# A layernorm + MLP kernel: the first weight piece moves from SP's DMA queue to ACT's, and four matmuls move ahead of the third tile's transposes

## The chip, the cores and the metric

The kernel runs on one core of a Trainium2 chip. The core has TensorE (PE: matmuls, and transposes as matmuls against an identity), VectorE (DVE), ScalarE (ACT), GpSimd (POOL) and SyncE (SP), and 16 DMA engines that all queues share. The metric is the device time of one execution in microseconds (us), lower is better; the time before is the median of 3 runs.

## What is computed

```python
def reference(x, w1, b1, w2, b2):            # x 1x2048x1024, w1 1024x3584, w2 3584x1024, all bf16
    y = _layernorm(x, axis=-1)
    h = _gelu(jnp.einsum("bsd,df->bsf", y, w1) + b1)
    return jnp.einsum("bsf,fd->bsd", h, w2) + b2
```

## The kernel before

**Tiling.** The 2048 rows of x are 16 tiles of 128 rows, in four blocks of 512 rows (four tiles). D = 1024 is 8 slices of 128 (`dt`), F = 3584 is 28 rows of 128 (`r`). For each block, the first matmul makes 28 rows of hT (128 features x 512 tokens), each accumulated over 8 `dt` in one PSUM bank; ACT applies gelu; the second matmul accumulates the 28 rows into 128x512 output pieces, DVE adds b2 and SP stores.

**The queues.** The program is five hand-ordered lists of instructions, one per engine; each instruction carries the events that it waits for. An engine never overtakes its own list. DVE's list in the steady part is put together by a planner from estimated ready times (`est`), which sums of matmul times and DMA bytes feed.

**The start.** PE runs 25 matmuls on a constant (L471), transposes b1 (L512), and then the first three tiles of x, which are multiplied raw, without their layernorm ("RAW", tiles 0, 1, 2); mean and rstd are put right afterwards on DVE (L529, L536, L539). `pe_T` (L320) transposes one tile in 8 transposes (L336, 128x128 each) into two PSUM banks, and ACT copies each bank to `yT_sb` (L352); tiles 0 and 1 are cut 4 + 4, tile 2 is cut 2 + 6. Tile 2 uses the banks of tile 0 again ("t" and "2_0"), so it waits for ACT's copies of these.

**The wave.** Then the first eight rows of hT are made as "cells" (`pe_wave`, L389, matmul L397): one cell is one row r and one slice dt over some tiles. A cell over tiles 0 and 1 has 258 columns (two columns of ones among them), over tile 2 128, over all three 386. The first weight piece, `w0`, holds rows 0 to 3 of dt 0 (128 KB), `w1` the same rows of dt 1, `w2` of dt 2 and 3, and so on (`PIECES`). Of piece 0 the four cells of tiles 0 and 1 come first, then the four of tile 2 (L564 to L567); all later pieces are cells of three tiles (L568), row by row. Tile 3 follows with 64 cells of 128 columns from its own normalised copy, and then come full rows (L382, 512 columns).

**The loads.** SP issues, in this order: x0, x1, x2 (256 KB each), w0, w1 (128 KB each), w2, w3, x3 (256 KB each) and so on; b1 (7 KB) alone is issued on ACT's queue (`issue`, L212; the DMA itself is recorded at L189). POOL's first instructions make the identity, a few constants and, for every tile, two memsets (L243, L244; the last is the event `eps15`).

**ACT's list at the start:** table load, b1's DMA, the copy of b1 out of PSUM (L516), the six copies of transposed tiles (L352), then the spreading of the means (L486), which waits for DVE until 11.2 us.

## Time and profile before

| | |
|---|---|
| median of 3 runs | 396.61 us (396.26 to 396.75) |
| the profiled execution: its time, its span | 396.67 us, 395.4 us |
| PE busy in the span | 390.9 us (99%) |
| DVE, ACT, POOL busy | 162.0, 86.2, 11.7 us |
| mean granted TensorE clock | 1.00 |
| first tile landed, first tile transposed, first cell | 3.5, 3.71, 6.38 us |

The span runs from the first recorded instruction to the last; 1.27 us of the execution lie outside it. Times in the timeline count from the start of the span. A timeline row is a start, a length to the end of the last instruction in the row, engine, line, operation, out<-in, shape and count. Matmuls overlap: one of 128 columns is recorded as 0.2 to 0.3 us long, so PE's pace is read from the distances of starts and not from lengths.

### The profile page before, as it was taken

How to read it: one execution, taken by the hardware profiler on the slowest of the kernel's cores; microseconds unless marked ns; L12 is line 12 of the kernel's file. 1: busy time of each engine (PE TensorE's matmuls, PEld its weight loads, DVE VectorE, ACT ScalarE, POOL GpSimd, SP SyncE). 2: the span in 40 equal slices, each digit the busy share in tenths (PEclk: the TensorE clock that was granted, in tenths of full speed). 3: DMA queues.
4: the chain of work that ended last, by engine and by line, in shares of the span. 5: the costliest groups of instructions: out<-in, count | busy, mean ns of one | idle time of the engine just before them, and what ended most of it. 6: DMA issues, size and time to landing. Idle time of an engine off the chain costs nothing.

```text
span 395.4 us, 4518 instructions
## 1 busy us (share of the span) xinstructions
PE 390.9 (99%) x1904; PEld 184.9 (47%) x1938; DVE 162.0 (41%) x338; ACT 86.2 (22%) x139; POOL 11.7 (3%) x59
## 2 busy tenths in 40 slices
PE   9999999999999999999999999999999999999998
PEld 7744444444444444444444444444444444444444
DVE  5998889988999306987100000001100000001011
ACT  3655420000144332000023443100003334400000
POOL 3101000011001100000000000000000000000000
DMA  7999940000000000000000000000000000000000
GB/s 257 373 385 386 387 155 26 16 27 14 28 0 0 2 0 0 28 26 15 28 13 2 0 0 2 13 13 28 25 15 15 0 0 2 0 15 27 13 28 27
DMA packets 16078, 23.63 MB, mean 60 GB/s; under 512 B 1082, under 2 KB 8250, under 8 KB 16058
## 3 DMA queue, kind: packets, MB, share of 16 engines
q1 hardware_dynamic: 16016, 23.33, 16.7%
q8 instruction: 15, 0.25, 0.3%
q14 instruction: 5, 0.04, 0.0%
q10 hardware_dynamic: 42, 0.01, 0.0%
HBM read 19.14 MB, written 4.19 MB: 59 GB/s over the span
## 4 chain that ended last, share of the span: by engine, by line
PE 99%; issue 0%; DVE 0%
PE ps L449 49%; PE ps L382 38%; PE ps_t L382 7%; PE ps L397 3%; PE ps L471 1%; PE ps_t L397 0%; PE ps L336 0%; PE ps_t L336 0%; DVE o_sb L460 0%; PE ps L512 0%
## 5 line engine op out<-in xcount | busy, mean ns | idle before, releaser
L449 PE MATMUL ps<-w_sb,hT_sb 128*128 128x512 bf16 (+2 forms) x909 | 193.3, 373 | 0.8
L382 PE MATMUL ps<-yT_sb,w_sb 128*128 128x512 bf16 x678 | 152.4, 379 | 0.9
L449 PEld LDWEIGHTS ps<-w_sb,hT_sb 128*128 128x128 bf16 x924 | 88.6, 98 | 105.2
L407 ACT ACTIVATE hT_sb<-ps,b_sb 128x512 bf16<-128x512 f32 x94 | 64.0, 687 | 234.4 <-PE ps L382 217.2
L382 PEld LDWEIGHTS ps<-yT_sb,w_sb 128*128 128x128 bf16 x696 | 68.0, 98 | 81.9
L460 DVE TENSOR_TENSOR o_sb<-ps,b_sb 128x512 bf16<-128x512 f32 (+2 forms) x33 | 22.3, 675 | 198.7 <-PE ps L449 198.5
L304 DVE STREAM_TRANSPOSE yT_sb<-x_sb 32x256 bf16<-32x256 bf16 x192 | 83.7, 436 | 21.9 <-PE ps_t L382 18.8
L382 PE MATMUL ps_t<-yT_sb,w_sb 128*128 128x512 bf16 x135 | 31.9, 379 | 0.1
L248 DVE BATCH_NORM_STATS2 st_sb<-x_sb 128x6 f32<-128x512 bf16 x32 | 21.0, 672 | 4.7 <-DMA x_sb<-in_x_dram 4.6
L382 PEld LDWEIGHTS ps_t<-yT_sb,w_sb 128*128 128x128 bf16 x136 | 13.3, 98 | 16.1
L407 ACT ACTIVATE hT_sb<-ps_t,b_sb 128x512 bf16<-128x512 f32 x18 | 12.4, 687 | 17.5 <-PE ps_t L382 14.6
L397 PE MATMUL ps<-yT_sb,w_sb 128*128 128x128 bf16 (+2 forms) x116 | 13.1, 269 | 0.0
L397 PEld LDWEIGHTS ps<-yT_sb,w_sb 128*128 128x128 bf16 x116 | 8.9, 98 | 3.5
L255 POOL TENSOR_TENSOR rstd_sb<-mv_sb,nhalf 128x1 f32<-128x1 f32 x13 | 7.1, 548 | 113.6 <-DVE mv_sb L258 113.6
L423 DVE TENSOR_TENSOR ps<-ps,row_r 128x384 f32<-128x384 f32 x17 | 9.2, 561 | 2.7 <-PE ps L382 2.5
L262 DVE TENSOR_SCALAR x_sb<-x_sb,mv_sb,rstd_sb 128x1024 bf16<-128x1024 bf16 x13 | 7.0, 541 | 2.0 <-POOL rstd_sb L255 1.3
L536 DVE SCALAR_TENSOR_TENSOR ps<-row_r,ncs,ps 128x384 f32<-128x384 f32 x7 | 4.2, 614 | 0.6 <-PE ps L397 0.6
L486 ACT COPY row_r<-row_r 32x384 f32<-32x384 f32 x6 | 3.1, 510 | 4.3 <-DVE row_r L480 4.2
L539 DVE TENSOR_TENSOR ps<-ps,row_r 128x384 f32<-128x384 f32 x7 | 3.9, 563 | 0.2
L529 DVE TENSOR_TENSOR yT_sb<-yT_sb,row_r 128x768 bf16<-128x768 bf16 x4 | 3.6, 950 | 0.0
L471 PE MATMUL ps<-const-bfloat16-1.0 128*128 128x128 bf16 x25 | 2.8, 309 | 0.8 <-PEq L679 0.8
L258 DVE BATCH_NORM_AGGREGATE mv_sb<-st_sb 128x2 f32<-128x15 f32 x13 | 2.9, 222 | 0.4
(34 smaller groups left out, 32.9 us busy)
## 6 DMA issues: line engine op xcount, KB each, us to landing
w_sb<-in_w_dram SPq DMA_DIRECT2D x4, 1792.0 KB, 18.3
w_sb<-in_w_dram SPq DMA_DIRECT2D x2, 2048.0 KB, 16.4
out_dram<-o_sb SPq DMA_DIRECT2D x31, 128.0 KB, 1.7
x_sb<-in_x_dram SPq DMA_DIRECT2D x3, 1024.0 KB, 14.4
w_sb<-in_w_dram SPq DMA_DIRECT2D x7, 256.0 KB, 5.4
x_sb<-in_x_dram SPq DMA_DIRECT2D x4, 256.0 KB, 3.4
w_sb<-in_w_dram SPq DMA_DIRECT2D x1, 1024.0 KB, 10.1
w_sb<-in_w_dram SPq DMA_DIRECT2D x2, 128.0 KB, 3.7
```

The costliest lines, as they stand in the source:

```text
L248: return (lambda e, i=i, h=h, pw=pw: e.bn_stats(st_sb[i][:, 6 * h:6 * (h + 1)], x_sb[:, i, h * pw:(h + 1) * pw]), [x_ev[i][h if len(x_ev[i ...
L255: pool.op(lambda e, i=i, dst=dst, mv=mv: e.tensor_tensor(out=dst, in0=mv[:, 1:2], in1=nhalf[:, i:i + 1], op=ALU.pow), waits=[f"mv{i}", "nh ...
L262: return (lambda e, i=i, c0=c0, c1=c1: e.tensor_scalar(out=x_sb[:, i, c0:c1], in0=x_sb[:, i, c0:c1], scalar1=mv_sb[:, i, 0:1], scalar2=rst ...
L304: res.append((lambda e, src=src, dst=dst: e.transpose(out=dst, in_=src), waits, (f"tr{i}" if lastop else None), 0.47))
L382: pe.op(lambda e, b=b, r=r, dt=dt, bank=bank: e.matmul(unit_bank(bank)[:, 0:TB], lhsT=w1_sb[:, dt, r * P:(r + 1) * P], rhs=yT_sb[:, ybuf(b ...
L397: pe.op(lambda e: e.matmul(unit_bank(bank)[:, n0:n1], lhsT=w1_sb[:, dt, r * P:(r + 1) * P], rhs=yT_sb[:, 0 if tiles[0] in RAW else ybuf(0) ...
L407: act.op(lambda e, r=r, n0=n0, n1=n1, bank=bank: e.activation(out=hT_sb[:, r, n0:n1], in_=unit_bank(bank)[:, n0:n1], func=ACT.Gelu_apprx_tanh,
L423: crit.append((est[sig], (lambda e, reg=reg: e.tensor_tensor(out=reg, in0=reg, in1=row_b(1), op=ALU.mult), [sig, "row_1"], ready, 0.57), 0))
L449: pe.op(lambda e, sl=sl, ft=ft, c0=c0, c1=c1, bank=bank: e.matmul(ps_2[:, bank, 0:c1 - c0], lhsT=hT_sb[:, ft, sl * P:(sl + 1) * P], rhs=w2 ...
L460: crit.append((est[sig], (lambda e, ob=ob, c0=c0, c1=c1, bank=bank: e.tensor_tensor(out=o_sb[:, ob, c0:c1], in0=ps_2[:, bank, 0:c1 - c0], ...
L471: pe.op(lambda e: e.matmul(ps_1[:, 0, 0:P], lhsT=ones, rhs=ones, start=True, stop=True))
L536: return [(lambda e: e.scalar_tensor_tensor(out=reg, in0=row_b(0), scalar=ncs[:, c:c + 1], in1=reg, op0=ALU.mult, op1=ALU.add), [f"m1_0_{r ...
```

## The change

- `w0` is issued on ACT's queue and not on SP's, behind b1's DMA, and it waits for POOL's last start-up memset (`eps15`). SP's queue issues x0, x1, x2, w1 and so on, all behind x2 one place earlier.
- Tiles 0 and 1 are cut 2 + 6 as tile 2 is. ACT's copies are ordered by piece: first piece of tile 0, first of tile 1, second of tile 0, second of tile 1.
- PE's order becomes: transposes of tiles 0 and 1; the four cells of dt 0 over tiles 0 and 1; the transposes of tile 2; the four cells of dt 1 over tiles 0 and 1; eight cells of tile 2 (dt 0 and 1); then cells of three tiles from dt 2 on. In before, dt 1 had cells of three tiles.
- Inside a piece the cells go slice by slice (all rows of one dt, then the next dt), and no more row by row.

```diff
-GROUPS_0 = (0, 4, 8)
-GROUPS_2 = (0, 2, 8)
+GROUPS = (0, 2, 8)
...
+N_EARLY = 1
+N_PAIR = 2
...
-SP_FIRST_LOADS = ("b1", "x0", "x1", "x2", "w0", "w1", "w2", "w3", "x3", "w4", "w5", "w6", "w7", "w8")
+SP_FIRST_LOADS = ("b1", "x0", "x1", "w0", "x2", "w1", "w2", "w3", "x3", "w4", "w5", "w6", "w7", "w8")
...
-                load_w1(int(item[1:]))
+                dma_q[0] = act if item == "w0" else sp
+                load_w1(int(item[1:]), [f"eps{NT - 1}"] if item == "w0" else [])
+                dma_q[0] = sp
...
+        def put_copy(i, groups, banks, k):
+            g0, g1 = groups[k:k + 2]
+            bname = banks[k]
+            assert banks.count(bname) == 1
+            src = bank_of[bname][:, 0:(g1 - g0) * P].bitcast(I32)
+            src = src.rearrange("p (j s) -> p j s", j=g1 - g0)
+            dst = yT_sb[:, 0, g0:g1, ycol(i):ycol(i) + P].bitcast(I32)
+            act.op(lambda e, dst=dst, src=src: e.copy(out=dst, in_=src), waits=[f"tp{i}_{k}"], sig=f"te{i}_{k}")
+            bank_read[bname] = f"te{i}_{k}"
...
-        pe_T(0, GROUPS_0, ("t", "2_0"))
-        pe_T(1, GROUPS_0, ("2_1", "1_4"))
-        pe_T(2, GROUPS_2, ("t", "2_0"))
-        put_row_spread(0, 1, 4)
+        T_BANKS = (("t", "2_0"), ("2_1", "1_4"), ("t", "2_0"))
+        for t in RAW[:2]:
+            pe_T(t, GROUPS, T_BANKS[t])
+        for k in range(2):
+            for t in RAW[:2]:
+                put_copy(t, GROUPS, T_BANKS[t], k)
...
-        first = [(r, dt) for r in PIECES[0][2] for dt in range(*PIECES[0][:2])]
-        for tiles in (RAW[:2], RAW[2:]):
-            for r, dt in first:
-                wave_cell(r, dt, tiles)
-        cells = [(r, dt) for j0, j1, rows in PIECES[1:] for r in rows if r < R for dt in range(j0, j1)]
+        cells_of = lambda a, b: [(r, dt) for j0, j1, rows in PIECES[a:b] for dt in range(j0, j1) for r in rows]
+        for r, dt in cells_of(0, N_EARLY):
+            wave_cell(r, dt, RAW[:2])
+        pe_T(2, GROUPS, T_BANKS[2])
+        for k in range(2):
+            put_copy(2, GROUPS, T_BANKS[2], k)
+        put_row_spread(0, 1, 4)
+        for r, dt in cells_of(N_EARLY, N_PAIR):
+            wave_cell(r, dt, RAW[:2])
+        for r, dt in sorted(cells_of(0, N_PAIR), key=lambda c: (c[1] >= GROUPS[1], c)):
+            wave_cell(r, dt, RAW[2:], f"raw_{r}" if dt == DT - 1 else None)
+        cells = cells_of(N_PAIR, len(PIECES))
```

More of the change, by code (lines that the diff above doesn't have):

```diff
@@ L117, in bass_standalone__mixer_channel_mlp__prompt_kernel @@
     assert NB1 + NB2 + 1 <= 8 and NB2 == 2
-    assert all(c[-1] == DT for c in (GROUPS_0, GROUPS_2, HALVES))
+    assert all(c[-1] == DT for c in (GROUPS, HALVES))
     assert TPB == 4 and RAW == (0, 1, 2)
@@ L201, in load_x_block, with load_w1 @@
                 x_ev[i] = (f"xb{b}", f"xb{b}")
-        def load_w1(ci):
+        def load_w1(ci, waits=()):
             j0, j1, a, b = w1_chunks[ci]
-            dma(w1_sb[:, j0:j1, a:b], w1v[:, j0:j1, a:b], f"w1c{ci}", (j1 - j0) * P * (b - a) * 2)
+            dma(w1_sb[:, j0:j1, a:b], w1v[:, j0:j1, a:b], f"w1c{ci}", (j1 - j0) * P * (b - a) * 2, waits)
             w1_issued.add(ci)
@@ L340, in pe_T @@
                     off += P
-            off = 0
-            prev = None
-            for k, (g0, g1) in enumerate(zip(groups[:-1], groups[1:])):
-                bname = banks[k]
-                if bname != prev:
-                    off = 0
-                prev = bname
-                done = max(m for m in range(len(banks)) if banks[m] == bname)
-                src = bank_of[bname][:, off:off + (g1 - g0) * P].bitcast(I32)
-                src = src.rearrange("p (j s) -> p j s", j=g1 - g0)
-                dst = yT_sb[:, 0 if i in RAW else ybuf(blk), g0:g1, ycol(i):ycol(i) + P].bitcast(I32)
-                act.op(lambda e, dst=dst, src=src: e.copy(out=dst, in_=src), waits=[f"tp{i}_{done}"],
-                       sig=f"te{i}_{k}")
-                off += (g1 - g0) * P
-                bank_read[bname] = f"te{i}_{k}"
-            pe_t[0] += DT * 0.056
+            pe_t[0] += DT * 0.056
+        def put_copy(i, groups, banks, k):
[7 more added lines that the diff above has]
+            bank_read[bname] = f"te{i}_{k}"
         unit_n = [0]
```

## Prediction, made before the result was known

> **What bounds the kernel now.** The page's chain of work first: it says which engine the end hangs on.

> ```profile
> ## 4 chain that ended last, share of the span: by engine, by line
> PE 99%; issue 0%; DVE 0%
> ```

> PE alone. So an edit is worth what it changes in PE's stream: a stall, or the pace. Next PE's timeline, to find where the stream isn't dense.

> ```profile
> 0.83 2.82 PE L471 MATMUL ps<-const-bfloat16-1.0 128*128 128x128 bf16 x25 [0.83 <-PEq L679]
> 3.58 0.20 PE L512 MATMUL ps<-ident,b1r_sb 28*128 28x28 bf16 x1
> 3.71 0.61 PE L336 MATMUL ps_t<-ident,x_sb 128*128 128x128 bf16 x4
> 4.11 1.49 PE L336 MATMUL ps<-ident,x_sb 128*128 128x128 bf16 x12
> 5.71 0.37 PE L336 MATMUL ps_t<-ident,x_sb 128*128 128x128 bf16 x2
> 5.87 0.67 PE L336 MATMUL ps<-ident,x_sb 128*128 128x128 bf16 x6
> 6.38 6.38 PE L397 MATMUL ps<-yT_sb,w_sb 128*128 128x258 bf16 x42
> ...
> 16.52 0.49 PE L397 MATMUL ps_t<-yT_sb,w_sb 128*128 128x386 bf16 x2
> 16.84 3.29 PE L397 MATMUL ps<-yT_sb,w_sb 128*128 128x128 bf16 x56
> 19.97 0.61 PE L397 MATMUL ps_t<-yT_sb,w_sb 128*128 128x128 bf16 x8
> ```

> Three readings, from starts. (a) Pace: the 12 transposes at 4.11 have 11 steps in 1.49 - 0.31 = 1.18 us, 107 ns for 128 columns; the 56 cells of 16.84 to 19.97 take 56 ns for as many columns. PE begins at half its later pace. The six transposes from 5.87 to 6.38 took 0.51 us: a of them at 107 and 6 - a at 56 gives a = 3.4, so the pace doubles at 5.87 + 3.4 x 0.107 = 6.23 us. The profile's column for the granted clock says 1.00 there, so only the steps show it. (b) One stall: the 16 transposes of tiles 0 and 1 would be followed by the next at 5.39 (3.71 + 16 steps, the first ones a little short); it comes at 5.71. (c) From 6.38 on nothing is lost: 34 cells of 386 columns at 163 ns, 4 of 258 at 110 and 4 of 128 at 56 are 6.2 us, and the row lasts from 6.38 to 12.60. Beyond that the steps stay 56 and 216 ns to the last matmul. So the change can act only on the first 6.4 us.

> What ended the stall, and whether it was the DMA: the queue and ACT.

> ```profile
> 1.69 0.42 SPq L189 DMA_DIRECT2D x_sb<-in_x_dram  x1
> x_sb<-in_x_dram SPq DMA_DIRECT2D x1, 256.0 KB, 3.9
> ...
> 2.15 0.43 SPq L189 DMA_DIRECT2D w_sb<-in_w_dram  x1
> w_sb<-in_w_dram SPq DMA_DIRECT2D x1, 128.0 KB, 3.8
> ```

> The first pair is x2: issued at 1.69, landed 3.9 later, 5.6. PE's next transpose starts 0.13 after that, while the bank that it also waits for had been copied by 4.73 (ACT's first copy, below). The stall is x2's. The second pair is w0: 2.15 + 3.8 = 5.95, needed at 6.38.

> ```profile
> 4.36 0.37 ACT L352 COPY yT_sb<-ps_t 128x256 int32<-128x256 int32 x1 [0.36 <-PE ps_t L336]
> 4.79 1.23 ACT L352 COPY yT_sb<-ps 128x256 int32<-128x256 int32 x3
> 6.11 0.27 ACT L352 COPY yT_sb<-ps_t 128x128 int32<-128x128 int32 x1
> 6.58 0.48 ACT L352 COPY yT_sb<-ps 128x384 int32<-128x384 int32 x1 [0.20 <-PE ps L336]
> ```

> **The change, part by part.**

> Transposes and copies. The same 24 transposes. Copies of tiles 0 and 1: four of 0.37 become two of 0.27 and two of 0.48, the same 1.5 us. By the same delays as in the rows above (0.04 behind PE, 0.05 apart) they run 4.15 to 4.41, 5.00 to 5.26, 5.31 to 5.79, 5.85 to 6.33. Tiles 0 and 1 have dt 0 in `yT_sb` at 5.26, before PE is through with their transposes (5.39): no wait. Tile 2 needs "2_0" free, 5.79, and will come later than that.

> w0 on ACT's queue. It waits for POOL's last memset, 2.29 + 0.09 = 2.38, and so is issued at about 2.42. ACT's one other issue took 0.62 us; the copy of b1 at 3.82 stands behind it, and ACT had 1.75 us idle before that: hidden, with 0.8 us of cover. SP's issues behind x2 start 0.47 earlier; the 16 DMA engines are full (DMA share 1.03 between 2.82 and 6.24), so bytes and not issues set when w1 and the rest land. I put this at nothing: no cell of these pieces waited.

> When w0 lands is the unknown price. Early end: 2.42 + 2.7, what x0 took with nothing ahead, = 5.1. Late end: 2.42 + 3.9, x2's own, = 6.3; short of that, 5.95 is where it lands today. With x1's 2.9 it would be 5.3. I take 5.4: nothing stands ahead on its queue, as with x1, but it shares the engines with the rest of x1 and with x2. x2 is then late by w0's share, 5.95 at most, as the two together are the bytes that are in by then today.

> [...]

> PE's new stretch. Let s be the start of the first early cell: the later of 5.39 and w0's landing + 0.13. From s to the end of piece 1, PE has 4 cells of 258 (0.44 us), 8 transposes (0.45), 4 cells of 258 (0.44), 8 cells of 128 (0.45): 1.78 us at full pace, and what runs before 6.23 goes at half. So the end is 6.23 + 1.78 - (6.23 - s)/1.95. In before the same point is 6.38 + 0.44 + 0.22 + 4 x 0.163 = 7.69.
> - w0 by 5.26: s = 5.39, end 7.58, gain 0.11.
> - w0 at 5.4: s = 5.54, end 7.65, gain 0.04.
> - w0 at 5.95: s = 6.08, end 7.93, loss 0.24.
> - w0 at 6.3: s = 6.45, end 8.23, loss 0.54.
> - No gain and no loss at w0 = 5.5.

> The gain is small for a plain reason: the stall that goes lies in the stretch of half pace, where 0.32 us of idle time are 0.16 us of work; and the cells put into it run at 215 ns and not at 110.

> Waits further on. With s = 5.54, the cells end at 6.32 and tile 2's transposes run 6.32 to 6.77, behind x2 (5.95 at most): its wait is gone. Its copies run 6.62 to 6.89 and 6.95 to 7.43; the cells that need them start at 7.21 and 7.65. Hidden, with 0.2 us of cover. w2 (landed 3.10 + 3.9 = 7.0) is needed at 7.65.

> Slice-by-slice order: the same cells. A change of bank costs no more than none: 163 ns holds for piece 1, which changes bank each cell, as for the pairs in one bank later. Row 0's end signal comes up to 1 us later, but ACT's reader waits for the last row anyway and stands behind copies that end at 12.8. Zero. Splitting dt 1's four cells costs 4 x (110 + 56 - 163) = 0.01, in the sum. The planner's estimates move by 0.01 us: at worst a few DVE instructions trade places, and PE waited for none of them in before.

> Later covers that a PE earlier by 0.1 us eats into: tile 3's copies end at 15.9, needed 16.8; the last bank of the wave is read by 28.76 and written again at 29.05. Both hold, so the gain reaches the end.

> **Sum.** Against the profiled execution: 396.67 - 0.04 = 396.63. It stands 0.06 above the median of 396.61, so against the median 396.57. What a measurement of this kernel can tell from no change is about 0.2%, 0.79 us; the whole bracket lies inside that.

> **The rivals.**

> 1. ACT's queue brings w0 no earlier than SP's did (the change doesn't do what it says). For: engines full, and issued 0.27 later than on SP. Against: b1's small load on that queue was in before PE asked for it at 3.58, while x1's load stood on SP's. Loss 0.24 (5.95) to 0.54 (6.3): 396.85 to 397.15. Chance 0.2.

> 2. The pace doubles sooner. Then w0 alone sets s: 5.54 + 1.78 = 7.32, gain 0.37, 396.24; with w0 at 5.1, s = 5.25, 7.03, gain 0.66, 395.95. For: the runs differ by 0.49 us with no stall beyond 6.4 to vary. Against: one trace, one doubling. Chance 0.14. [...]

> 3. The other side: the wait for w0 is long enough that PE doesn't count as busy, and the pace doubles later. PE had run 5.4 us (0.83 to 6.23), idle 0.45 of them, when it doubled. If a stall of 0.7 or more (w0 later than about 6.0) starts that count again at s = 6.2, the doubling comes at 11.6, and half of 11.6 - 6.23 is lost: 2.7 us, 399.3. For: half pace at first, so something is counted. Against: the 0.32 stall at 5.39 didn't prevent it, and w0 must be later than today. Chance 0.06. [...]

> **Numbers.** Forecast (w0 by 5.5, doubling near 6.2) 0.60, rivals 0.20, 0.14, 0.06. Faster by over 0.2% needs more than any case but an early doubling with an early load would give: 0.03. Slower: rival 3 and the tail of rival 1: 0.07. Same: 0.90. Range 396.0 to 397.0: from rival 2 to most of rival 1.

> **What would show it.** Step 1: w0's issue on ACT at 2.4 and landing 2.7 to 3.5 later. Step 2: no gap between the 16th transpose and the first cell of 258 columns beyond 0.2, at steps of 215 ns. Step 3: eight transposes behind the cells at 56 ns and no gap before them. Step 4: the first cells of 386 columns at 7.6 to 7.7 in place of 7.04 + 0.65. It would be wrong if the pace doubles elsewhere than at 6.0 to 6.5, if w0 lands after 5.6, or if PE waits anywhere beyond 8 us.

## The result, and the profile after

The changed kernel is slower by 0.3%: 397.12 us against 396.48 us (medians of 22 executions each); the ratio of the means is 1.0029, 95% interval 1.0018 to 1.0040. The forecast was 396.57 and no measurable difference.

The 22 executions fall into two groups, with nothing between 397.23 and 398.61. Fifteen lie at 396.86 to 397.23 (median 397.04, 0.56 above before); seven lie at 398.61 to 399.05 (median 398.90, 1.86 above the first group). Before had none of 22 there. The two together give the mean: 0.56 + 7/22 x 1.86 = 1.15 us, as 397.61 - 396.48 = 1.13. All 22 count in the comparison; what makes the second group is the subject of half the experiments. The profiled execution, 397.13 with a span of 395.9, belongs to the first; none of the second was traced. Its mean granted clock is known, though: 0.996 in two of the seven (399.01 and 399.05), 1.00 in the other five, as in all of the first group.

The page's chain of work, in 4, now holds a DMA:

```profile
PE 98%; DMA 1%; POOL 0%; issue 0%; DVE 0%; POOLq 0%
PE ps L447 49%; PE ps L380 38%; PE ps_t L380 7%; PE ps L395 3%; DMA w_sb<-in_w_dram 1%; PE ps_t L395 0%; POOL st_sb L247 0%; POOL st_sb L246 0%; PE ps L339 0%; POOL ident L239 0%; DVE o_sb L458 0%; PE ps_t L339 0%; POOL yT_sb L242 0%; POOL nhalf L243 0%; POOLq L239 0%
```

The chain in order of time says which DMA (start, length, what):

```profile
2.41 3.85 DMA w_sb<-in_w_dram
6.26 0.14 issue
6.40 0.60 PE ps L395 x4
```

That is w0: issued on ACT at 2.41 behind POOL's last memset (the small POOL entries above), landed at 6.26, and the early cells start at 6.40. PE's timeline of the same stretch, to be laid beside the one of before:

```profile
3.90 1.70 PE L339 MATMUL ps<-ident,x_sb 128*128 128x128 bf16 x14
6.40 0.60 PE L395 MATMUL ps<-yT_sb,w_sb 128*128 128x258 bf16 x4 [0.80 <-DMA w_sb<-in_w_dram]
6.84 0.27 PE L339 MATMUL ps_t<-ident,x_sb 128*128 128x128 bf16 x2
6.95 0.50 PE L339 MATMUL ps<-ident,x_sb 128*128 128x128 bf16 x6
7.28 5.46 PE L395 MATMUL ps<-yT_sb,w_sb 128*128 128x258 bf16 x39
```

Behind the 16th transpose PE could have gone on at 5.39; it stands until 6.40 (the 0.80 counts from the end of that transpose). In before the same place cost 0.31. The steps ahead of the wait are at half pace (the 14 transposes, 107 ns each), those behind it at full pace (the four cells 6.40 to 6.84, 110 ns each; the transposes behind them 56): the doubling fell into the wait. The first cell of 386 columns starts at 8.17, with the work done that before had done at 7.69 (its point behind piece 1): 0.48 later, and this stays to the last matmul (0.47).

### The profile page after: what moved, and what is told of

Its sections match the earlier page's. It is cut to its first block, busy times and chain, and to the rows that moved or that the text cites. A ratio compares the mean times of both kernels' runs of the same rounds, so it can differ in the third digit from the quotient of the medians.

```text
span 395.9 us, 4560 instructions
## 1 busy us (share of the span) xinstructions
PE 392.5 (99%) x1942; PEld 185.0 (47%) x1942; DVE 162.0 (41%) x338; ACT 86.1 (22%) x139; POOL 11.7 (3%) x59
## 4 chain that ended last, share of the span: by engine, by line
PE 98%; DMA 1%; POOL 0%; issue 0%; DVE 0%; POOLq 0%
PE ps L447 49%; PE ps L380 38%; PE ps_t L380 7%; PE ps L395 3%; DMA w_sb<-in_w_dram 1%; PE ps_t L395 0%; POOL st_sb L247 0%; POOL st_sb L246 0%; PE ps L339 0%; POOL ident L239 0%; DVE o_sb L458 0%; PE ps_t L339 0%; POOL yT_sb L242 0%; POOL nhalf L243 0%; POOLq L239 0%
## 5 line engine op out<-in xcount | busy, mean ns | idle before, releaser
L395 PE MATMUL ps<-yT_sb,w_sb 128*128 128x128 bf16 (+2 forms) x120 | 13.9, 266 | 0.8 <-DMA w_sb<-in_w_dram 0.8
L395 PE MATMUL ps_t<-yT_sb,w_sb 128*128 128x386 bf16 (+1 forms) x16 | 3.2, 273 | 0.0
## 6 DMA issues: line engine op xcount, KB each, us to landing
w_sb<-in_w_dram SPq DMA_DIRECT2D x2, 2048.0 KB, 15.9
out_dram<-o_sb SPq DMA_DIRECT2D x31, 128.0 KB, 1.7
w_sb<-in_w_dram SPq DMA_DIRECT2D x7, 256.0 KB, 5.3
x_sb<-in_x_dram SPq DMA_DIRECT2D x4, 256.0 KB, 3.1
b_sb<-in_b_dram SPq DMA_DIRECT2D x1, 256.0 KB, 14.4
```

What stands on the lines that cost most here:

```text
L395: pe.op(lambda e: e.matmul(unit_bank(bank)[:, n0:n1], lhsT=w1_sb[:, dt, r * P:(r + 1) * P], rhs=yT_sb[:, 0 if tiles[0] in RAW else ybuf(0) ...
```

## The experiments

"Before" is the kernel before, run in the same rounds: 396.63 us (35 executions) beside e1 to e4, 396.69 (29) beside e5 to e8, 396.50 (23) beside e9 to e12. Over all these and the first 22 it had 4 of 109 executions above 398.2. Landings are each kernel's profiled execution's.

**e1: w0 earlier, on ACT's queue**

```diff
-                load_w1(int(item[1:]), [f"eps{NT - 1}"] if item == "w0" else [])
+                load_w1(int(item[1:]))
```

> The changed kernel, with w0 on ACT's queue but no wait for POOL's memset. Theory A (loads land in the order in which both queues issued them, at the pace of the bytes; PE then idles at half pace, and sometimes the pace doubles a whole period later): w0 is issued at 1.4 to 1.5 us, between x1 and x2, and lands at 4.4 to 4.9; x2 lands at 5.0 to 5.6; the first early cell starts at 5.39 with no idle time; no execution stands near 398.9, and the median is 396.3 to 396.5, 0.0 to 0.2 under the kernel before. Rival B (ACT's queue is slow of itself, 3.85 us from issue to landing as in the changed kernel): w0 lands at 5.3, the first cell starts at 5.4, about the same time; only the landing tells A from B. Rival C (the new order of PE's work, not w0's lateness, costs the time): 397.0 and a third of the executions near 398.9, as in the changed kernel.

Measured: 396.33 (395.81 to 396.85, 12 executions), ratio 0.9993 (0.9983 to 1.0003); w0 issued at 1.47, landed at 4.79, x2 at 5.19. No execution in an upper group. Rival C falls: PE's new order costs nothing that shows when w0 is there. The profiled execution, the fastest, shows one way in which executions differ:

```profile
3.68 0.29 PE L339 MATMUL ps_t<-ident,x_sb 128*128 128x128 bf16 x2
3.81 0.94 PE L339 MATMUL ps<-ident,x_sb 128*128 128x128 bf16 x14
4.97 0.60 PE L395 MATMUL ps<-yT_sb,w_sb 128*128 128x258 bf16 x4 [0.22 <-DMA w_sb<-in_w_dram]
```

Fourteen transposes in 0.94 us, 55 ns from start to start, against 1.70 and 107 above: the pace had doubled by 3.8 and not at 6.2, with the same 25 matmuls ahead. Then w0's landing sets the first cell, as in the prediction's second rival.

**e2: w0 earlier, on SP's queue between x1 and x2**

```diff
-                dma_q[0] = act if item == "w0" else sp
-                load_w1(int(item[1:]), [f"eps{NT - 1}"] if item == "w0" else [])
-                dma_q[0] = sp
+                load_w1(int(item[1:]))
```

> The changed kernel, with w0 on SP's queue between x1 and x2. Theory A: issued at about 1.69, landed at 4.4 to 4.9, x2 at 5.0 to 5.6, no idle time ahead of the first early cell, median 396.3 to 396.5, no upper group. Rival B (ACT's queue is slow): this one lands 0.5 or more earlier than in the run without the wait. Rival C (PE's order costs it): 397.0 with a third near 398.9.

Measured: 396.65 (396.19 to 398.81, 12), ratio 1.0000 (0.9985 to 1.0015), one execution in the upper group; issued at 1.69, landed at 5.24, x2 at 5.90. Not the gain that was expected, but rival B falls: SP's queue needed 3.55 us from issue to landing, ACT's in e1 3.33.

**e3: the waiting time filled**

```diff
+        warm(8)
         for r, dt in cells_of(0, N_EARLY):
```

> The changed kernel with eight more matmuls on the constant (128 columns, 107 ns each at half pace) on PE between tile 1's transposes and the first early cell, where PE idles 0.80 us. They do no work of the reference. Theory A (the late doubling of the pace comes from PE's idle time): the upper group near 398.9, 7 of 22 executions of the changed kernel, is gone; all executions lie at 396.8 to 397.3, median 397.0; w0 still lands near 6.2. Rival D (the upper group has another cause, such as a DMA on ACT's queue or the order of the cells): about a third of the executions stay near 398.9.

Measured: 397.41 (397.01 to 397.68, 12), none above. No execution is in the upper group, as theory A has it. The level is 0.4 above what was expected; in the profiled execution w0 landed at 6.60 and PE waited 0.49 us more behind the eight matmuls.

**e4: the queue alone.** The kernel before, with w0 on ACT's queue as in the changed one.

```diff
-                load_w1(int(item[1:]))
+                dma_q[0] = act if item == "w0" else sp
+                load_w1(int(item[1:]), [f"eps{NT - 1}"] if item == "w0" else [])
+                dma_q[0] = sp
```

> The kernel before with w0 alone moved to ACT's queue with the wait for POOL; PE's and ACT's order as before. Theory A: w0 lands at 6.2 to 6.3 and is needed at 6.38, so that the first cell starts at 6.38 to 6.45: 396.4 to 396.6, equal to before within 0.1, no upper group. Rival D (a DMA on ACT's queue at this place makes the upper group): a third near 398.9. Rival B's own reading (queue slow of itself) gives the same landing here.

Measured: 396.98 (396.44 to 399.44, 12), ratio 1.0015 (0.9999 to 1.0031), three above 398.4. The expectation fails, and rival D gets a point. The trace of one of the three (398.46) is to hand: x2 landed at 5.94, PE stood from 5.40 to 6.08, and then the pace did not double. Two answers for cells of 386 columns, 8.5 to 9.4 and 9.7 to 12.0 us (lengths in ns: shortest, median, longest; then the first and the last start):

```profile
L399 PE MATMUL ps<-yT_sb,w_sb x4: 528/528/528, 8.2 to 9.1; 128*128 128x386 bf16 x4
```

```profile
L399 PE MATMUL ps<-yT_sb,w_sb x16: 327/327/372, 9.5 to 12.0; 128*128 128x386 bf16 x16
```

From start to start these are 0.3 us a cell and then 0.17. The cells go at half pace until about 9.5 us, 3.3 later than before's 6.23. That is one way in which an execution comes into the upper group.

**e5: the order alone.** The changed kernel with w0 on SP behind x2.

```diff
-SP_FIRST_LOADS = ("b1", "x0", "x1", "w0", "x2", "w1", ...
+SP_FIRST_LOADS = ("b1", "x0", "x1", "x2", "w0", "w1", ...
```

(The lines of e2's diff as well.)

> The new order of PE's and ACT's work alone: w0 back on SP's queue behind x2, where it stood in the kernel before. Theory A (PE's idle time ahead of the early cells, set by when w0 lands, is the price; a long one also makes the pace double a period later in some executions): w0 lands at 5.9 to 6.5, PE idles 0.6 to 1.2 us behind the 16th transpose, the lower group lies at 396.7 to 397.1, and 1 to 5 of 12 executions lie near 398.8. Rival E (the loss came from the move to ACT's queue): 396.3 to 396.6 with no upper group.

Measured: 396.84 (396.41 to 397.19, 11), ratio 1.0001 (0.9990 to 1.0012); w0 landed at 6.23, PE stood from 5.40 to 6.36. No execution above. The level is as expected, the missing upper group is not.

**e6: before, held for w1**

```diff
+                    if i == 2 and j == 0:
+                        waits.append("w1c1")
```

> The kernel before with one wait more: the first transpose of tile 2 waits for w1 as well, which it does not need. PE's order, ACT's order and the queues are those of before. Theory A: PE idles 0.7 to 1.3 us at the place where the changed kernel idles; the lower group lies at 396.9 to 397.2 and 2 to 6 of 12 executions lie near 398.8. Rival D (the upper group comes from the new order of cells or from a DMA on ACT's queue): the lower group alone, and not more near 398.8 than the 3 of 57 of the kernel before.

Measured: 397.34 (396.95 to 398.85, 12), ratio 1.0018 (1.0010 to 1.0027); PE stood from 5.40 to 6.57; one of 12 above, and seven of the lower eleven above the 397.2 that was expected. With nothing of the change in the kernel, an idle PE alone costs as much as the lower group of the changed kernel pays (0.65 us by medians, against 0.56). On the upper group e5 and e6 lean to rival D: 1 of 23.

**e7: the changed kernel, held longer**

```diff
+        pe.op(None, waits=["w1c2"])
         for r, dt in cells_of(0, N_EARLY):
```

> The changed kernel with its first early cell held until w2 has landed (7.0 to 7.9 us), so that PE's idle time doubles from 0.8 to 1.6 or more. Theory A: the lower group moves up by the longer wait to 397.7 to 398.3, the upper group stays at 398.8 to 399.3 (its doubling comes at the same time, near 9.5 us), and it holds more than half of the executions against a third. Rival D (the share of the upper group does not hang on idle time): a third as before.

Measured: 398.01, 398.08, 398.12, 399.96, 399.97 and 400.19: half of six, too few to tell from a third or from more than half; the upper ones are later than expected. The trace (an upper one) shows a second way into the upper group. PE's timeline, and its stretches (from and to, length, PE busy and count, granted clock, DMA share, GB/s):

```profile
3.90 1.31 PE L339 MATMUL ps<-ident,x_sb 128*128 128x128 bf16 x14
7.58 0.61 PE L395 MATMUL ps<-yT_sb,w_sb 128*128 128x258 bf16 x4 [2.36 <-DMA w_sb<-in_w_dram]
8.03 0.36 PE L339 MATMUL ps_t<-ident,x_sb 128*128 128x128 bf16 x2
8.19 0.84 PE L339 MATMUL ps<-ident,x_sb 128*128 128x128 bf16 x6
```

```profile
4.72:5.10 0.38, 0.38 (x9) 1.00 0.85 310
7.70:8.05 0.35, 0.35 (x5) 1.00 0.94 337
8.20:11.40 3.20, 3.20 (x23) 0.50 1.08 371
11.60:12.50 0.90, 0.90 (x8) 1.00 1.10 348
```

The pace had doubled at 4.7, PE stood from 5.1 until 7.58, ran four cells at full pace, and at 8.09 fell back to half: here the granted clock says so, 0.50. It doubled again at 11.50. From 4.68 to 8.09 and from 8.09 to 11.50 is 3.41 us each.

**e8: the early load alone.** e4 without the wait, so that before's order has w0 issued at 1.47.

```diff
-                load_w1(int(item[1:]), [f"eps{NT - 1}"] if item == "w0" else [])
+                load_w1(int(item[1:]))
```

> PE's and ACT's order of the kernel before, with w0 on ACT's queue and no wait for POOL (issued at 1.47, as in the run without the wait). Theory A: w0 lands near 4.8 and nobody needs it before 6.4; x2, with its bytes behind w0's, lands 0 to 0.4 later than on average before, so tile 2's transposes wait as long or longer: 396.5 to 396.9, not under the kernel before; what the run without the wait wins needs PE's new order. Rival F (the early load itself makes the time better): 396.2 to 396.4.

Measured: 396.49 (396.17 to 396.92, 11), ratio 0.9994 (0.9985 to 1.0002). Between the two expectations: not told from before. w0 landed at 5.43 and x2 at 5.62; with the same issue time, 1.47, w0 had landed at 4.79 in e1.

**e9: the changed kernel again,** with no edit.

> The changed kernel once more, on the same chip and in the same rounds as the two held kernels, since their shares of late executions are to be compared. Theory A: lower group 396.9 to 397.2, 2 to 6 of 12 executions at 398.6 to 399.1. If it has none here, the share hangs on the day as much as on the kernel.

Measured: 397.14 against 396.50, ratio 1.0018 (1.0005 to 1.0031); nine at 396.84 to 397.24, two at 398.90 and 399.25; w0 landed at 6.27.

**e10: before, held longer**

```diff
-                        waits.append("w1c1")
+                        waits.append("w1c2")
```

(On top of e6.)

> The kernel before with the first transpose of tile 2 held until w2 has landed (7.0 to 7.6), which it does not need: PE idles 1.6 to 2.2 us, with PE's order, ACT's order and the queues of before. Theory A (a stretch with too much idle time leaves PE at half pace for one more period): lower group 397.6 to 398.3, and 4 to 8 of 12 executions 1.5 to 2.0 above it, as in the changed kernel held to the same load (3 of 6). Rival D (the upper group needs the DMA on ACT's queue or the new order): at most 1 of 12 above 399.

Measured: 398.03, 398.91, 399.46, 399.54, 399.73, 401.14: four of six above 399; 398.91 and 401.14 lie in neither of the two groups that were expected. The profiled one (398.03) stood from 5.40 to 7.31. Rival D falls as the only cause: neither ACT's queue nor the new order is in this kernel.

**e11: the longer hold, filled**

```diff
+        warm(20)
         pe.op(None, waits=["w1c2"])
```

(On top of e7.)

> The changed kernel held to w2, as in the run that had 3 of 6 executions near 400, with 20 more matmuls on the constant in the waiting time (they do no work of the reference; 2.1 us at half pace). Theory A: nobody above 399.0; all at 397.6 to 398.3, the lower group of the held run. Rival D: half of them near 400 again.

Measured: 397.98 (397.65 to 398.52, five executions). The same hold, and nobody above 399; 398.52 lies above the expected group. The filling was not complete: in the trace the 20 matmuls ran at full pace (58 ns each), and PE still stood from 6.1 to 7.19.

**e12: e1 with 27 matmuls on the constant**

```diff
-N_WARM = 25
+N_WARM = 27
```

> The run without the wait (w0 on ACT's queue at 1.47, PE's new order) with 27 in place of 25 matmuls on the constant, so that PE's 0.25 us of idle time ahead of the first tile shrink to under 0.1. Theory A: the stretch that decides on the pace holds less idle time, the pace doubles 0 to 0.2 earlier: 396.2 to 396.4, under the kernel before by 0.2 to 0.4. If b1's and tile 0's transposes are pushed back instead: 396.4 to 396.5.

Measured: 396.56 (396.01 to 396.89, 11), ratio 0.9997 (0.9988 to 1.0006). The idle 0.25 us stayed, only later: b1's transpose moved from 3.58 to 3.80. Nearer to the second expectation. No version tried here is clear of the kernel before.

## Why the prediction was wrong, point by point

**What bounds the kernel, and the place.** Right: every difference lies ahead of 8.2 us; beyond it the steps are 56, 163 and 216 ns in both traces.

**When w0 lands: the step that failed.** The prediction took 5.4, from x1's 2.9 us, because "nothing stands ahead on its queue". It landed at 6.26 in the profiled execution and at 6.27 in e9, near the late end of the bracket (6.3, x2's own 3.9 us). An empty queue bought nothing. Two stretches of the changed kernel's DMA view, 2.9 to 4.3 and 4.3 to 5.9 us (packets, MB, share of the engines; q1 is SP's, q10 ACT's):

```profile
q1 hardware_dynamic: 308, 0.54, 105.9%
```

```profile
q1 hardware_dynamic: 363, 0.35, 68.7%
q10 hardware_dynamic: 144, 0.13, 30.4%
```

w0 was issued at 2.41; until 4.3 not one packet of it moved, while what SP had issued earlier filled the engines. Then it shared them with w1, issued at 2.15, and landed 0.23 behind it (in e4, e7 and e11 0.2 ahead of it). The late start is not special to this kernel: w0's first packet of 1 KB moved 1.8 to 2.2 us behind its issue in all nine traces with w0 on ACT's queue (issued at 1.47 or 2.41) and 1.8 to 2.1 in the five with it on SP's (at 1.69 or 2.15), where x0's first packet came 1.0 behind its issue. x0's 2.7 therefore did not hold for w0. What x1's 2.9 left out is in the main the sharing: w0's 128 KB moved from 4.40 to 5.72, 1.3 us, where x1's 256 KB, begun 1.75 behind its issue, took about 0.65 (2.96 to 3.62). The prediction had put at nothing that SP's loads behind x2 start 0.47 earlier; it is w1, in w0's old slot, and w2 behind it that w0 shared the engines with.

Over all traces w0 took 3.2 to 4.2 us from issue to landing on ACT's queue and 3.6 to 4.1 on SP's: the moment of the issue counts, and no difference between the queues shows. The wait for POOL's memset put that moment at 2.41, behind SP's old slot at 2.15, and w0 landed at 6.12 to 6.63 in the six traces with this slot against 5.94 to 6.23 in the four with the old one. So the likely case was the prediction's first rival, chance 0.2.

With less issued ahead the delay was about as long: e1's w0, with only x0, x1 and b1 ahead of it, also began 1.9 us behind its issue, and then had 73% of the engines from 3.4 to 3.9. What makes the 2 us is not shown.

**The price of a late w0.** Right: for w0 at 6.3 the prediction's formula gives s = 6.45 and a loss of 0.54; the first group lost 0.56, the first cell of 386 columns 0.48.

**x2.** "Late by w0's share" was not seen in the changed kernel's two traces (4.94, and 5.17 in e9, against 5.6 in before), but in the four others with the same loads (e3, e4, e7, e11: 5.94 to 6.38). With one issue time, 1.69, x2 landed at 4.94 to 6.38 over all traces; the prediction took its one landing as given.

**When the pace doubles.** The third rival was right that the pace can double later behind a longer wait (e4: near 9.5 behind a wait until 6.08, before: at 6.23 behind one until 5.71); its chance of 0.06 was low for what came in 9 of 33 executions of the changed kernel (7 of 22, 2 of 11). Its price of 2.7 us was too high, since it started the count at the end of the stall. Measured: 1.86. The traces show two periods, both in e7 and both of 3.41 us; by them half pace for one period more is an estimated 3.41/2 = 1.7 us. And the pace doubled by 3.8 (e1), at 4.7 (e7) and at 6.2 (before) behind the same first matmul at 0.8 and the same 25 matmuls: what PE had done by 3.6 does not fix the moment.

By the mean clocks, both ways into the upper group occur in the changed kernel. A period of 3.41 us at a granted clock of 0.50 makes the mean of some 398 us 0.996, as in e7's three upper executions; three of the nine (two, and one of e9's) read 0.996, and six read 1.00, as e4's traced one does, in which the first doubling came late.

How much idle time is too much can only be argued, with e7's 3.41 us taken for the period of the other traces too: before's 3.41 us ahead of its doubling at 6.23 hold 0.56 us without a step of PE, and the pace doubled; e4's ahead of 6.1, one period short of 9.5, hold about 0.9, and it didn't. The changed kernel's 1.0 us, with the 0.25 ahead of 3.7, lies beyond both; yet behind as long a wait its profiled execution and those of e5, e6 and e10 ran at full pace, and in e9's the pace had doubled at 5.2 and a wait of 1.1 us behind that did not take it back. So where in a period the wait falls should count too; that is argued. What is shown is this: holding PE without the change makes the upper group (e10: four of six above 399, where before had none of 109), and with the wait filled it was not seen (e3, e11: none of 12 and none of 5; at a share of 9 in 33, none of 12 is a chance of 0.02).

**Open.** e5 and e6 stood as long as the changed kernel (0.96 and 1.18 us in their profiles) and had 1 of 23 above against 9 of 33. The chance of so few at equal shares is about 0.03. Whether that is chance, shorter waits in the other executions, a part of ACT's queue in it, or the chip was not settled: e5 to e8 ran on another chip than e1 to e4, and e9 to e12 on a third; the changed kernel as it is was not run beside e5 and e6. Why one load lands at different times with the same issue time (x2 up to 1.4 us, w0 up to 0.8) was not tried.

**The gain.** The prediction's best case, 0.11 for w0 by 5.26, was not refuted: e1, where w0 landed at 4.79, stands 0.30 under before, with an interval from 0.67 under to 0.12 above. e12, with w0 at 4.65, stands 0.06 above, so a gain is not shown either. The parts alone cost 0.35 (e4) and 0.15 (e5) by medians, neither clear of before by itself; that they add up to the lower group's 0.56 is not shown.

## What to carry to other kernels

Here a load was early when it was issued early: on an idle queue behind a wait w0 was issued at 2.41 and landed at 6.12 to 6.63, in its old place in a busy queue it was issued at 2.15 and landed at 5.94 to 6.23. Moving work ahead of a wait can pay only if its own operand beats that wait in the late executions too; compare landing times over several traces (x2's, with one issue time, were 4.94 to 6.38), and not one. And idle time in the first microseconds of PE's stream cost more than its length in some executions here: the changed kernel, whose profile has 1.0 us of it behind the 16th transpose, lost 0.56 us in 15 of the first 22 executions and 2.42 in seven. With that wait filled none of 12 was in the upper group (e3): fill it, or look for a second group in the times.
